# Attention and two feed-forward layers on one core: the order of an attention round written anew on every engine queue

## The chip, the cores and the metric

One core of a Trainium2 chip runs the whole program in one launch. The metric is the device time of a run in microseconds (us); lower is better. The kernel before takes 1006.01 us, the median of three runs.

## What is computed

Causal attention with a decay over 4 batches of 8 heads, 576 positions, 64 values a head, then two feed-forward layers over the 2304 tokens. All in float32, so most products are made of three (high times high, high times low, low times high).

```python
scores = (1 / 8) * q @ k.T                      # per head, 576 x 576
cum = cumsum(log(clip(f, 1e-4, 1)))
scores = where(causal, -1e9, scores + cum[:, None] - cum[None, :])
attn = exp(scores - max) ; attn = attn / (sum(attn) + 1e-9)
x = attn @ v                                    # as (2304, 512)
h = x @ w_in ; x = (h * cos(h)) @ w_out         # layer one, 512 -> 2048 -> 512
y = (silu(x @ w_gate) * (x @ w_val)) @ w_out2   # layer two, 512 -> 1536 -> 512
```

## The kernel before, in words

The program has three stages on one set of engines: attention, layer one, layer two. The change touches attention and the seam to layer one.

Attention works on 16 pairs of heads (index i), both heads of a pair side by side in the partitions (e = 0, 1). The 576 positions are cut into five tiles of queries t: 128 each, 64 in the last. Each pair passes through small steps, which the text names as the program's table does:

- `q0` to `q3` (emit_q, L117 and L114, POOL): split q and k of the pair into a rounded high part and the rest, into the tile xq. `qb` (emit_b) lays a block diagonal bd for tile 4 and a selector that adds the decay.
- `S4, S1, S2, S0, S3` (emit_s, L412 to L421, PE): score products of a tile into the PSUM tiles sA (S4, later S0 and S2 together) and sB (S1, later S3). The last product of each adds the decay: its weights are the selector, its moving side the cumulated logarithms cs.
- `M` (emit_m, L436, DVE): masks the scores, takes them out of PSUM into P (tile 4: Q), and gives the row maximum. M40 is that of tile 4. `E` (emit_e, L444, ACT): exponential with the row's sum.
- `T0` to `T3` (emit_t, L481, PE): transposes of the probabilities into a PSUM tile t; there are two such tiles. `C` (emit_c, L502 on ACT, L500 on DVE): copies out of it to pt. Which copies are DVE's is the table CPD.
- `ra, rb, rt, rc, rd, re, rf` (emit_recip): the reciprocal of the sums, transposed, to DRAM (r_d) and read back over all partitions (rs).
- `V0, V1` (emit_pv, L535, PE): probabilities times values, one half of the columns each, into the two halves of one t tile. `N0, N1` (emit_n, L544, DVE): times the reciprocals. `xo`: the result to DRAM.
- `wd, w1` to `w7` (w_load, w_step): prepare one weight tile of layer one in each round, beside attention. w1 is an absolute value on ACT (L167), w2 a clamp (L169), w3 two shifts (L171), w4 and w5 put the bits together (L173, L175), w6 rounds on POOL (L117) and w7 takes the rest on POOL (L114).

What sets the order is one string, SCH: a list such as `M40@1`, which means that in round n the step M40 of pair n - 1 stands here. The loop at the end of attention runs through the list once a round (21 rounds), and `in_order` fixes that every engine keeps the order in which its instructions were recorded. So each engine has a fixed queue, and a step that waits holds all that stands behind it on its engine. FIRST and AHEAD give the first pairs another order. A t tile becomes free when its readers are done; a wait for it is a wait for the whole tile.

Layer one (in1, out1) begins behind attention: for each of 16 blocks j of the hidden size a product h (L252, 12 matmuls), a cosine over ACT and DVE, and two steps later the product with w_out (L694). Its first block of tokens is loaded and split (xh, xl) on POOL in the last rounds: XL, XP and XN say when and how many splits at a time.

Of the kernel before, what the change touches and what calls it, by code (L numbers as in the profile page):

```python
# [9 lines left out]
F32 = mybir.dt.float32  # L10
F32R = mybir.dt.float32r
# [15 lines left out]
CH = 384  # L27
# [69 lines left out]
def body(ctx: ExitStack, tc: tile.TileContext, qk, v, f, w_in, w_out, w_gate, w_val, w_out2, mask_c, ident_c, sel_c, out):  # L97
# [56 lines left out]
    def w_step(n, k):  # L154

        raw, ta = wcur[n][:2]
        w32 = raw.bitcast(I32).rearrange("p (c two) -> p c two", two=2)
        lo, hi = w32[:, :, 0], w32[:, :, 1]  # L160
        if k == 1:
            sp = stages[0] if n < SA else stages[1]
            while n >= SB and held[0] > TAB2 - 2:
                small.pop(0)[1]()
            ta = wcur[n][1] = sp.tile([128, 512], I32, tag="ta", name="ta", bufs=TAB if n < SA else TAB2)
            hi32 = raw.bitcast(F32).rearrange("p (c two) -> p c two", two=2)[:, :, 1]
            ACT.activation(out=ta.bitcast(F32), in_=hi32, func=AF.Abs)  # L167
        elif k == 2:
            DVE.tensor_scalar(out=ta.bitcast(F32), in0=ta.bitcast(F32), scalar1=HI_MIN, scalar2=HI_MAX, op0=ALU.max, op1=ALU.min)  # L169
        elif k == 3:  # L170
            DVE.tensor_scalar(out=ta, in0=ta, scalar1=5, scalar2=2, op0=ALU.logical_shift_left, op1=ALU.logical_shift_right)  # L171
        elif k == 4:
# [215 lines left out]
    def s_place(i, t):  # L388
        if i < 2 and t in (1, 4):
# [8 lines left out]
    def emit_s(i, t):  # L398
        s = sels[i % 3]
        if i > 1 or i == 1 and t in (1, 4):  # L400
# [5 lines left out]
        if t < 4:  # L406
# [11 lines left out]
        for m, (x, y) in enumerate([*((x, y) for _, y, x in p), (s[:, 64:192], None)]):  # L418
            for g in range(2):
# [30 lines left out]
    def emit_recip(i, k):  # L450
# [42 lines left out]
    def emit_c(i, g, e):  # L493
# [10 lines left out]
        n = 4 - g  # L504
        if g < 2:
# [3 lines left out]
        for e in range(2):  # L509
            if g == 2:  # L510
                copy(o[:, e, PJ[g]:PJ[g] + 128 * n].rearrange("p (n h x) -> p n h x", n=n, h=2),
                     ps[:, :, 64 * n * e:64 * n * e + 64 * n].rearrange("p h (n x) -> p n h x", n=n))
        if g == 3:
# [44 lines left out]


    def op(o, i):  # L560

        if not 0 <= i < NPAIR:
            return
        if i in FIRST and o[0] in "SME":
            now = [int(t[0]) for t in FIRST[i].split()]
            slot = [4, 1, 2, 0, 3]
            k = slot.index(int(o[1]))
            if o[0] == "S":
                o = f"S{now[k]}"
            else:  # L570
                flat = {x: [f"{t}{e}" for t in x for e in range(2 if t != 4 else 1)] for x in (tuple(now), tuple(slot))}
                o = o[0] + flat[tuple(now)][flat[tuple(slot)].index(o[1:])]
        if (o, i) in BEHIND:
# [58 lines left out]

    sch = [t.split("@") for t in SCH.split()]
# [481 lines left out]
```

## Time and profile before

| | |
|---|---|
| three runs | 1004.76, 1006.01, 1006.56 us |
| the profiled execution | 1007.36 us |
| its span, first to last instruction | 1005.6 us |
| busy: PE, DVE, ACT, POOL | 96%, 74%, 51%, 46% of the span |
| mean granted clock of TensorE | 0.983 of 2.4 GHz |
| attention | about the first 205 us |

The shares are means over three stages. From 211 us on PE runs without a gap; the idle time of PE lies in attention, so that stage is to be read by itself, by rounds.

### The profile page before, as it was taken

Reading aid. Unit: us, or ns where it says so; the run is one execution under the profiler, and the core shown is the slowest. Engines: PE = TensorE matmul, PEld = TensorE weight load, DVE = VectorE, ACT = ScalarE, POOL = GpSimd, SP = SyncE. Lnnn points to the kernel's source line nnn. Section 1 sums busy time; section 2 is a strip of 40 time slices with the busy share of each in tenths; the row PEclk is TensorE's granted clock in tenths of the full one; section 3 lists DMA queues with packets and bytes.
Section 4 is the critical chain, followed back from the end, with each engine's and each line's share of the span. In section 5 each row is a group of like instructions: output and inputs, shape, how many; then the busy total and the mean of one; then the engine's idle time right before and its main releaser. Section 6 shows DMA issues by size and latency. Waiting matters only on the chain.

```text
span 1005.6 us, 18021 instructions
## 1 busy us (share of the span) xinstructions
PE 960.7 (96%) x6522; PEld 903.7 (90%) x6522; DVE 744.8 (74%) x1311; ACT 507.9 (51%) x1122; POOL 466.8 (46%) x493
## 2 busy tenths in 40 slices
PE   8777878899999999999999999999999999999998
PEld 5666666599999999999999999999999999988888
DVE  6678777679788876979886653768576676898884
ACT  6767677645554555655655542324232331455552
POOL 7566665344225667769788002545553554200000
PEclk9989899899999999999999999999999999999999
DMA  4545443543345875967966776132961318954531
GB/s 160 178 161 196 158 171 128 174 156 129 105 147 189 251 219 179 302 211 239 290 226 219 252 251 223 55 118 78 350 219 56 118 48 312 363 188 138 157 105 43
DMA packets 108985, 182.61 MB, mean 182 GB/s; under 512 B 8912, under 2 KB 72800, under 8 KB 108896
## 3 DMA queue, kind: packets, MB, share of 16 engines
q1 hardware_dynamic: 108896, 181.46, 54.6%
q8 instruction: 51, 0.84, 0.3%
q14 instruction: 38, 0.31, 0.1%
HBM read 118.43 MB, written 62.99 MB: 180 GB/s over the span
## 4 chain that ended last, share of the span: by engine, by line
PE 79%; DVE 9%; DMA 4%; POOL 3%; issue 3%; ACT 2%; SPq 0%; DVEq 0%; POOLq 0%; ACTq 0%
PE h L252 15%; PE t L694 14%; PE b L885 11%; PE c L885 7%; PE a L885 7%; PE t L535 5%; PE b L974 5%; PE a L974 3%; DVE P L436 3%; PE sA L421 2%; PE c L974 1%; PE d L974 1%; PE sA L412 1%; DMA xl<-x 1%; PE t L481 1%
## 5 line engine op out<-in xcount | busy, mean ns | idle before, releaser
L252 PE MATMUL h<-xh,w 128*128 128x384 f32 x768 | 149.9, 335 | 1.5 <-POOL xh L117 1.5
L694 PE MATMUL t<-gh,w 128*128 128x384 f32 x704 | 137.1, 335 | 1.2 <-DVE part L704 0.9
L252 PEld LDWEIGHTS h<-xh,w 128*128 128x128 f32 x768 | 134.7, 188 | 2.3 <-POOL xh L117 1.9
L694 PEld LDWEIGHTS t<-gh,w 128*128 128x128 f32 x704 | 122.9, 188 | 2.8 <-DVE part L704 1.9
L885 PE MATMUL b<-c,wu 128*128 128x384 f32 x648 | 121.1, 334 | 0.0
L670 ACT ACTIVATE n<-h 128x384 int32<-128x384 f32 x96 | 47.2, 491 | 139.1 <-PE h L252 132.2
L885 PEld LDWEIGHTS b<-c,wu 128*128 128x128 f32 x648 | 113.1, 188 | 0.0
L672 DVE SCALAR_TENSOR_TENSOR r<-h,n 128x384 f32<-128x384 f32 x96 | 53.2, 554 | 74.0 <-ACT n L670 73.9
L848 POOL TENSOR_TENSOR s<-u,s 128x384 f32<-128x384 f32 x33 | 37.8, 1146 | 123.6 <-ACT s L847 117.1
L535 PE MATMUL t<-pt,vt 128*64 128x320 f32 (+4 forms) x448 | 61.6, 423 | 33.4 <-DVE xp L544 27.4
L535 PEld LDWEIGHTS t<-pt,vt 128*64 128x64 f32 x448 | 35.0, 157 | 59.4 <-DVE xp L544 31.3
L252 PE MATMUL h<-xl,w 128*128 128x384 f32 x384 | 82.0, 334 | 0.0
L885 PE MATMUL c<-c,wu 128*128 128x384 f32 x432 | 80.7, 334 | 0.0
L885 PE MATMUL a<-c,wu 128*128 128x384 f32 x432 | 80.7, 334 | 0.0
L885 PEld LDWEIGHTS c<-c,wu 128*128 128x128 f32 x432 | 75.4, 188 | 0.0
L885 PEld LDWEIGHTS a<-c,wu 128*128 128x128 f32 x432 | 75.4, 188 | 0.0
L694 PE MATMUL t<-gl,w 128*128 128x384 f32 x352 | 75.2, 334 | 0.0
L114 POOL TENSOR_TENSOR w<-ta,w 128x512 fp32r<-128x512 f32 x32 | 44.9, 1403 | 57.6 <-ACT w L189 29.4
L502 ACT COPY pt<-t 128x256 f32<-128x256 f32 (+2 forms) x109 | 42.4, 449 | 56.3 <-PE t L481 55.5
L444 ACT ACTIVATE P<-P,mx 128x384 f32<-128x384 f32 (+3 forms) x128 | 70.1, 549 | 0.2 <-DVE mx L436 0.2
L252 PEld LDWEIGHTS h<-xl,w 128*128 128x128 f32 x384 | 67.9, 188 | 0.0
L173 DVE SCALAR_TENSOR_TENSOR ta<-wraw,ta 128x512 int32<-128x512 int32 x68 | 66.0, 970 | 0.5
(160 smaller groups left out, 2113.4 us busy)
## 6 DMA issues: line engine op xcount, KB each, us to landing
wu<-wu SPq DMA_DIRECT2D x63, 512.0 KB, 5.0
wraw<-in_w_out_dram SPq DMA_DIRECT2D x28, 512.0 KB, 3.6
wu<-hi SPq DMA_DIRECT2D x54, 256.0 KB, 4.2
gd<-g SPq DMA_DIRECT2D x72, 192.0 KB, 2.4
gt<-gd SPq DMA_DIRECT2D x36, 384.0 KB, 5.7
raw<-in_qk_dram SPq DMA_DIRECT2D x16, 576.0 KB
wu<-sums SPq DMA_DIRECT2D x36, 256.0 KB, 3.3
xb<-x SPq DMA_DIRECT2D x24, 384.0 KB, 7.7
```

Source lines behind the costliest of these rows:

```text
L114: eng.tensor_tensor(out=o, in0=a, in1=b.bitcast(F32), op=ALU.subtract)
L173: DVE.scalar_tensor_tensor(out=ta, in0=lo, scalar=29, in1=ta, op0=ALU.logical_shift_right, op1=ALU.bitwise_or)
L252: PE.matmul(ps, lhsT=w[:, a, 128 * kk:128 * kk + 128], rhs=b[:, kk], start=(n == 0), stop=(n == 3 * KD - 1))
L444: ACT.activation(out=o, in_=o, func=AF.Exp, scale=-1.0, bias=mxt[p % 8][:, t:t + 1], accum_out=smt[p // 2 % 3][:, c:c + 1])
L502: ACT.copy(out=o, in_=x)
L535: PE.matmul(ps[64 * e:64 * e + 64, o:min(w, o + KW[j])], lhsT=vt_t[i][:, j, e], rhs=PT[i][:, e, c:c + w - o], start=(j == 0), stop=(j == b ...
L670: ACT.activation(out=n, in_=h, func=AF.Copy, scale=INV2PI, bias=0.25)
L672: DVE.scalar_tensor_tensor(out=r, in0=h, scalar=INV2PI, in1=n, op0=ALU.mult, op1=ALU.subtract)
L694: PE.matmul(acc[m][:, :CH], lhsT=wo[:, q, 128 * m:128 * m + 128], rhs=x, start=(j == a and n == 0), stop=False)
L848: e.tensor_tensor(out=s, in0=C[:, 0], in1=s, op=ALU.mult)
L885: PE.matmul(d, lhsT=wu[q, i][1][:, mem, x, 128 * kt:128 * kt + 128], rhs=r, start=bool(s and n == 0), stop=(n == 5), skip_group_check=True)
L974: PE.matmul(ot[:, :w], lhsT=cmb[i][:, x, q], rhs=m[:, 256 * y:256 * y + w], start=(i in (1, 5) and n == 0), stop=(n == len(ops) - 1), skip ...
```

## The change

Five things are changed together. (1) SCH is written anew: the same steps in another order, with other offsets (V and C30 one round earlier against the rest, N behind both halves of V, 20 rounds in place of 21); FIRST and AHEAD follow. (2) The clamp w2 goes from DVE to POOL for the weights prepared within attention. (3) Copy C21 goes from ACT to DVE (CPD). (4) The decay's selectors are no longer laid out per pair as 64x128 columns: one small tile holds a column per pair and head, and the products read it with step 0. Only tile 4 gets a laid out selector (sf, one POOL instruction). (5) The products h of layer one for j = 0 and j = 1 are issued ahead of T1 and V0 of the last pair, in PSUM that the scores have left; the splits of the first tokens start earlier for it.

```diff
-CPD = ("10", "11")
-SCH = "ld@-1 rd@3 xo@5 M30@2 M31@2 T0@3 q0@0 C00@3 C01@3 V0@4 w2@4 w3@4 q1@0 ...
+CPD = ("10", "11", "21")
+XH = {("T1", NPAIR - 1): 0, ("V0", NPAIR - 1): 1}
+SCH = "M21@2 w4@4 M31@2 q2@0 w5@4 N0@4 E30@2 ld@-1 N1@4 S4@1 T1@3 E00@2 re@3 rf@3 ...
...
-XL = 13
-XP = 14
-XN = 2
+XL = 10
+XP = 11
+XN = 1
...
         elif k == 2:
-            DVE.tensor_scalar(out=ta.bitcast(F32), in0=ta.bitcast(F32), scalar1=HI_MIN, ...
+            (POOL if n < SA else DVE).tensor_scalar(out=ta.bitcast(F32), in0=ta.bitcast(F32), scalar1=HI_MIN, ...
...
-    sels = [ap1.tile([128, 256], F32R, name=f"sel{k}") for k in range(3)]
+    sel = ap1.tile([128, NPAIR, 2], F32R, name="sel")
+    sel4s = [ap1.tile([128, 128], F32R, name=f"sf{k}") for k in range(2)]
...
-            pool_round(s[b, 128 * e:128 * e + 128], selr[b, i:i + 1].to_broadcast([64, 128]))
+        if i == 0:
+            for e in range(2):
+                b = slice(64 * e, 64 * e + 64)
+                pool_round(sel[b, :, e], selr[b, :NPAIR])
+        pool_round(sel4s[i % 2].rearrange("p (e x) -> p e x", e=2), sel[:, i, :, None].bitcast(F32).to_broadcast([128, 2, 64]))
...
-                PE.matmul(o[:, e], lhsT=s[b, 128 * e:128 * e + 128], rhs=cs[b, :ext], start=False, stop=True)
+                PE.matmul(o[:, e], lhsT=sel[b, i, e:e + 1].to_broadcast([64, 128]), rhs=cs[b, :ext], start=False, stop=True)
...
+    def ahead(j):
+        if "h" not in pools:
+            pctx.close()
+            pools["h"] = hctx.enter_context(tc.tile_pool(name="ps_h", bufs=4, space=PSUM))
+        h = hs[0, j] = pools["h"].tile([128, 512], F32, tag="h", name="h")[:, :CH]
+        mm_in(h, wt["i", j], xs[0])
...
     for n in range(NPAIR + moff):
         for o, off in sch:
+            if (o, n - int(off)) in XH:
+                ahead(XH[o, n - int(off)])
             op(o, n - int(off))
```

What stands where in a steady round, on three engines. First PE, at the values (V, the rows with pt and vt) of one pair, with the engines on whose semaphore a row waits. Before:

```order
L535 MATMUL t<-pt,vt 64x256 [waits DMAHW6_49,PE_49,Activation_49]
L535 MATMUL t<-pt,vt 64x256
L535 MATMUL t<-pt,vt 64x128 x2
L535 MATMUL t<-pt,vt 64x320 [waits DVE_49]
L535 MATMUL t<-pt,vt 64x320 x5
L535 MATMUL t<-pt,vt 64x192 x2
L535 MATMUL t<-pt,vt 64x64 x2
L421 MATMUL sA<-xq,bd_119 128x288 [waits Pool_49]
```

Now:

```order
L533 MATMUL t<-pt,vt 64x256 [waits DMAHW2_49,DVE_49,Activation_49]
L533 MATMUL t<-pt,vt 64x256
L533 MATMUL t<-pt,vt 64x128 x2
L533 MATMUL t<-pt,vt 64x320 x6
L533 MATMUL t<-pt,vt 64x192 x2
L533 MATMUL t<-pt,vt 64x64 x2
L423 MATMUL sA<-xq,bd_118 128x288 [waits DVE_49,Pool_49]
```

The second half (64x320 and on) waited for DVE and now waits for nothing; the wait for DVE stands at the first half and at S4 (the row with bd) behind it.

Second DVE, at the same place of the round (xp is N, ta the weight, the rows with mask are M, Q is M40). Before:

```order
L436 ISA P_110,mx_172<-sB,mask 128x512
L436 ISA mx_172 128x1
L169 TENSOR_SCALAR ta<-ta 128x512
L171 TENSOR_SCALAR ta<-ta 128x512
L544 TENSOR_TENSOR xp<-t,rs 128x256
L173 SCALAR_TENSOR_TENSOR ta<-wraw,ta 128x512
L544 TENSOR_TENSOR xp<-t,rs 128x320
L175 SCALAR_TENSOR_TENSOR ta<-wraw,ta 128x512
L436 ISA Q_116,mx_173<-sA,mask_99 128x576
```

Now:

```order
L438 ISA P_110,mx_170<-sA,mask 128x384
L438 ISA mx_170 128x1
L174 SCALAR_TENSOR_TENSOR ta<-wraw,ta 128x512
L438 ISA P_110,mx_170<-sB,mask 128x512
L438 ISA mx_170 128x1
L176 SCALAR_TENSOR_TENSOR ta<-wraw,ta 128x512
L542 TENSOR_TENSOR xp<-t,rs 128x256
L542 TENSOR_TENSOR xp<-t,rs 128x320
L438 ISA Q_116,mx_171<-sA,mask_99 128x576
```

The clamp is gone from DVE, w3 stands earlier in the round (behind the two M of tile 1), w4 and w5 stand ahead of N0, and N0 and N1 follow each other directly.

Third POOL, one round (rc is ra, ta the clamp, xq the splits of q and k, sel and sf the selectors). Before:

```order
L454 TENSOR_SCALAR rc_179<-sm_176 128x9
L117 TENSOR_SCALAR w_1969<-ta 128x512
L117 TENSOR_SCALAR sel_120<-selr 64x128 x2
L117 TENSOR_SCALAR bd_118<-xq 64x2x64 x2
L114 TENSOR_TENSOR w_1969<-ta,w_1969 128x512
L114 TENSOR_TENSOR xq<-raw,xq 128x576
L117 TENSOR_SCALAR xq<-raw 128x576
```

Now:

```order
L456 TENSOR_SCALAR rc_177<-sm_174 128x9
L170 TENSOR_SCALAR ta<-ta 128x512
L115 TENSOR_TENSOR xq<-raw,xq 128x576 x2
L118 TENSOR_SCALAR sf_121<-sel 128x128
L118 TENSOR_SCALAR bd_118<-xq 64x2x64 x2
L115 TENSOR_TENSOR w_872<-ta,w_872 128x512
L118 TENSOR_SCALAR xq<-raw 128x576 x2
L118 TENSOR_SCALAR w_1047<-ta 128x512
```

The clamp stands between ra and the two long splits; the selector is one instruction in place of two; the round of w (w6) stands at the end, ahead of the next ra.

## Rows read from the trace of the kernel before

**Rows 1.** The page, part 1: busy us, share of the span, instructions.

```profile
PE 960.7 (96%) x6522; PEld 903.7 (90%) x6522; DVE 744.8 (74%) x1311; ACT 507.9 (51%) x1122; POOL 466.8 (46%) x493
```

**Rows 2.** Busy time by stretch: length, five engines, PEclk, DMA share, GB/s.

```profile
42.70:163.15 120.45, 96.15 (x1201) 76.06 (x1201) 92.08 (x271) 84.86 (x273) 76.26 (x110) 0.93 0.49 166
114.96:127.83 12.87, 10.36 (x121) 8.12 (x121) 9.32 (x28) 8.58 (x29) 7.70 (x12) 0.87 0.46 160
127.83:138.99 11.16, 8.84 (x120) 7.21 (x120) 9.07 (x28) 8.36 (x28) 7.56 (x11) 1.00 0.56 192
...
178.45:211.28 32.83, 27.37 (x290) 20.33 (x291) 20.19 (x49) 16.99 (x48) 14.57 (x17) 0.90 0.46 153
```

**Rows 3.** Waits, 42.70 to 163.15 us: total, times, longest us.

```profile
POOL w L117 <- DVE ta L175: 23.7, 10, 3.4
PE t L535 <- DVE xp L544: 23.5, 11, 2.6
DVE xp L544 <- PE t L535: 23.3, 10, 3.3
```

**Rows 4.** Timeline of PE: start, us, instruction, count, idle before and releaser.

```profile
114.96 3.33 PE L535 MATMUL t<-pt,vt 128*64 128x320 f32 x20 [2.40 <-DVE xp L544]
...
127.83 2.28 PE L535 MATMUL t<-pt,vt 128*64 128x320 f32 x20 [2.50 <-DVE xp L544]
...
135.85 0.87 PE L535 MATMUL t<-pt,vt 128*64 128x256 f32 x8
```

**Rows 5.** Groups of DVE by shape, 42.70 to 163.15: busy us, mean ns, idle.

```profile
L171 DVE TENSOR_SCALAR ta<-ta 128x512 int32<-128x512 int32 x10 | 12.2, 1216 | 0.3
L500 DVE COPY pt<-t 128x384 f32<-128x384 f32 x20 | 10.1, 546 | 0.0
L173 DVE SCALAR_TENSOR_TENSOR ta<-wraw,ta 128x512 int32<-128x512 int32 x11 | 8.3, 751 | 0.0
L169 DVE TENSOR_SCALAR ta<-ta 128x512 f32<-128x512 f32 x10 | 7.9, 791 | 0.0
...
L175 DVE SCALAR_TENSOR_TENSOR ta<-wraw,ta 128x512 int32<-128x512 int32 x10 | 6.8, 682 | 0.0
```

**Rows 6.** Timelines of DVE (two rows) and POOL (the last), two rounds.

```profile
137.10 1.51 DVE L171 TENSOR_SCALAR ta<-ta 128x512 int32<-128x512 int32 x1
...
174.06 0.43 DVE L171 TENSOR_SCALAR ta<-ta 128x512 int32<-128x512 int32 x1
...
136.77 1.55 POOL L114 TENSOR_TENSOR xq<-raw,xq 128x576 fp32r<-128x576 f32 x1
```

**Rows 7.** Groups of POOL by shape, 40 to 180 us.

```profile
L117 POOL TENSOR_SCALAR w<-ta 128x512 fp32r<-128x512 f32 x12 | 7.5, 622 | 27.5 <-DVE ta L175 27.5
...
L117 POOL TENSOR_SCALAR sel<-selr 64x128 fp32r<-64x128 f32 x22 | 6.5, 295 | 0.7
```

**Rows 8.** Groups of weight loads by shape, 42.70 to 163.15 us.

```profile
L415 PEld LDWEIGHTS sA<-cs,sel 64*128 64x128 f32 x40 | 3.9, 186 | 0.0
```

**Rows 9.** Timeline of DVE where the first pair's values are done.

```profile
29.60 0.42 DVE L544 TENSOR_TENSOR xp<-t,rs 128x256 f32<-128x256 f32 x1 [1.76 <-DMA rs<-r_d]
33.88 0.49 DVE L544 TENSOR_TENSOR xp<-t,rs 128x320 f32<-128x320 f32 x1 [3.85 <-PE t L535]
35.28 0.76 DVE L436 CUSTOM_DVE_ANT_0 Q<-sA,mask 128x576 f32<-128x576 f32 x1 [0.92 <-PE sA L421]
```

**Rows 10.** The seam: timelines of DVE and PE, then POOL's splits (groups, 0 to 260).

```profile
178.45 0.76 DVE L436 CUSTOM_DVE_ANT_0 Q<-sA,mask 128x576 f32<-128x576 f32 x1 [0.17 <-PE sA L421]
...
205.45 1.14 PE L252 MATMUL h<-xh,w 128*128 128x384 f32 x5
...
211.28 1.61 PE L694 MATMUL t<-gh,w 128*128 128x384 f32 x8
...
L114 POOL TENSOR_TENSOR xl<-xl,xh 128x384 fp32r<-128x384 f32 x8 | 8.9, 1107 | 0.7
...
L117 POOL TENSOR_SCALAR xh<-xl 128x384 fp32r<-128x384 f32 x8 | 5.8, 721 | 11.5 <-DMA xl<-x 11.5
```

More of the change, by code (lines that the diff above doesn't have):

```diff
@@ L43 @@
 WHE = 1
-CPD = ("10", "11")
-FIRST = {0: "2 0 3 1 4", 1: "2 0 3 4 1"}
-SCH = "ld@-1 rd@3 xo@5 M30@2 M31@2 T0@3 q0@0 C00@3 C01@3 V0@4 w2@4 w3@4 q1@0 E20@2 E21@2 N0@4 E00@2 E01@2 w4@4 V1@4 E30@2 N1@4 E31@2 w1@3 w5@4 q2@0 S4@1 re@3 rf@3 ra@2 S1@1 M40@1 T3@3 M10@1 C30@3 M11@1 T1@3 rb@2 S2@1 C10@3 E40@1 C11@3 w6@4 S0@1 wd@2 lv@3 T2@3 rt@2 M20@1 C20@3 S3@1 rc@2 E10@1 M21@1 qb@0 E11@1 M00@1 w7@4 M01@1 q3@0 xk@3"
+CPD = ("10", "11", "21")
+FIRST = {0: "20314", 1: "32041"}
+XH = {("T1", NPAIR - 1): 0, ("V0", NPAIR - 1): 1}
+SCH = "M21@2 w4@4 M31@2 q2@0 w5@4 N0@4 E30@2 ld@-1 N1@4 S4@1 T1@3 E00@2 re@3 rf@3 q0@0 S1@1 xo@4 wd@2 E01@2 E10@2 M40@1 w6@4 T3@3 E21@2 E31@2 C10@3 S2@1 C11@3 w1@3 ra@2 S0@1 w2@3 q3@0 rb@2 M10@1 M11@1 T2@3 rt@2 C30@3 w3@3 q1@0 qb@0 C21@3 E40@1 T0@2 S3@1 rc@2 C20@3 rd@2 M20@1 M01@1 M00@1 C01@2 M30@1 V0@3 E11@1 V1@3 E20@1 w7@4 lv@2 C00@2 xk@3"
 JS = 9
@@ L168, in w_step @@
         elif k == 2:
-            DVE.tensor_scalar(out=ta.bitcast(F32), in0=ta.bitcast(F32), scalar1=HI_MIN, scalar2=HI_MAX, op0=ALU.max, op1=ALU.min)
+            (POOL if n < SA else DVE).tensor_scalar(out=ta.bitcast(F32), in0=ta.bitcast(F32), scalar1=HI_MIN, scalar2=HI_MAX, op0=ALU.max, op1=ALU.min)
         elif k == 3:
@@ L320, in body @@
     POOL.memset(mask4[:, 0:512], 0.0)
-    for b in (*sels, bd0, *bd):
+    for b in (bd0, sel, *bd):
         POOL.memset(b.bitcast(F32), 0.0)
@@ L363, in emit_q @@
     def emit_q(i, k):
-        if k == 0:
+        if i not in xq:
             xq[i] = aps.tile([128, 2, 2, S], F32R, tag="xq", name="xq", bufs=2)
@@ L388, in s_place @@
     def s_place(i, t):
-        if i < 2 and t in (1, 4):
+        if i == 0 and t in (1, 4) or i == 1 and t == 4:
             if (i, t) not in early:
@@ L414, in emit_s @@
                 b = slice(64 * e, 64 * e + 64)
-                PE.matmul(o[:, e], lhsT=s[b, 128 * e:128 * e + 128], rhs=cs[b, :ext], start=False, stop=True)
+                PE.matmul(o[:, e], lhsT=sel[b, i, e:e + 1].to_broadcast([64, 128]), rhs=cs[b, :ext], start=False, stop=True)
             return
         o = s_place(i, 4)
-        for m, (x, y) in enumerate([*((x, y) for _, y, x in p), (s[:, 64:192], None)]):
+        for m, (x, y) in enumerate([*((x, y) for _, y, x in p), (sel4s[i % 2], None)]):
             for g in range(2):
@@ L457, in emit_recip @@
         elif k == "t":
-            rps[i] = (tps[i - 1, 2][:9, :, 256:320] if i else t_tile()[:9, :, :64])
+            rps[i] = tps[i - 1, 2][:9, :, 256:320] if i else tps[0, 1][:9, :, 384:448]
             for h in range(2):
@@ L504, in emit_c @@
         n = 4 - g
-        if g < 2:
+        if g < 3:
             copy(o[:, e, PJ[g]:PJ[g] + 128 * n].rearrange("p (n h x) -> p n h x", n=n, h=2),
@@ L508, in emit_c @@
             return
[L509 to L512, printed above, removed]
         if g == 3:
@@ L557, in load_chunk, with flat @@
             xs[c] = load_x(xpools[c % 2], x1v, c % 2 * HT + c // 2 * CH, CH, GX and c == 1, later)
+    sch = [t.split("@") for t in SCH.split()]
+    SLOTS = {k: [t for _, _, t in sorted((int(f), n, t) for n, (t, f) in enumerate(sch) if t[0] == k)] for k in "SME"}
+    def flat(k, ts):
+        return [t + e for t in ts for e in ([""] if k == "S" else "0" if t == "4" else "01")]
     def op(o, i):
@@ L564, in op @@
         if i in FIRST and o[0] in "SME":
[L565 to L572, printed above, removed]
+            o = o[0] + flat(o[0], FIRST[i])[SLOTS[o[0]].index(o)]
         if (o, i) in BEHIND:
@@ L577, in op @@
         act(o, i)
-    AHEAD = {("M10", 1): (("ra", 0), ("rb", 0)), ("S4", 2): (("rt", 0), ("rc", 0), ("rd", 0)), ("T2", 0): (("re", 0), ("rf", 0))}
+    AHEAD = {("M10", 1): (("ra", 0), ("rb", 0)), ("C10", 0): (("rt", 0), ("rc", 0), ("rd", 0)), ("T0", 1): (("re", 0), ("rf", 0))}
     BEHIND = {a for b in AHEAD.values() for a in b}
@@ L631, in in_order @@
             last_[ins.engine] = ins
-    sch = [t.split("@") for t in SCH.split()]
+    def ahead(j):
[4 more added lines that the diff above has]
+        mm_in(h, wt["i", j], xs[0])
+    pools, hs = {}, {}
     moff = max(int(o) for _, o in sch)
@@ L651, in body @@
     stages[1] = rctx.enter_context(tc.tile_pool(name="stage2", bufs=RWB2, side=SIDE_R))
-    ps_h = hctx.enter_context(tc.tile_pool(name="ps_h", bufs=4, space=PSUM))
     G = {}
@@ L662, in in1 @@
         if k == 0:
-            h = ps_h.tile([128, 512], F32, tag="h", name="h")[:, :CH]
-            mm_in(h, wt["i", j], xs[c])
+            h = hs.pop((c, j), None)
+            if h is None:
+                h = pools["h"].tile([128, 512], F32, tag="h", name="h")[:, :CH]
+                mm_in(h, wt["i", j], xs[c])
             n = mp2.tile([128, CH], I32, tag="n", name="n")
```

5 lines of the change are left out of this document (removed).

## The prediction

> **What bounds the kernel now.** I read the page first: PE is busy for 96% of the span [rows 1]. That is a mean over three stages, so I cut attention into its rounds, from one start of V1 to the next. Ten rounds take 120.45 us, 12.05 each, and in them PE is busy for 9.6, DVE 9.2, ACT 8.5 and POOL 7.6 us a round [rows 2]. No engine is full; something goes round in a circle. The waits name it: PE's V1 waits for DVE's N0, 23.5 us in all, and DVE's N1 waits for V1, 23.3 us [rows 3], some 2.35 us a round each. The place in the queues explains it. V1 writes the second half of the tile that N0 reads, and was recorded behind N0; N0 stands behind all M of the round and the weight steps w2 and w3. So PE stands still until DVE has drained its list, then DVE stands still while PE does V1, S4 and so on. The round is the sum of both.
>
> The rounds come in two lengths, 11.16 and 12.9 us [rows 2]. In the long one V1 took 3.33 us in place of 2.28 [rows 4], and the granted clock of the round was 0.87, that is, part of it ran at 1.2 GHz in place of 2.4. Both had PE idle for about 2.4 us right before. A second thing lies in the weight steps: L171 took 0.43 us in one round and 1.51 in another, where POOL was inside a 1.55 us split that began 0.33 us earlier [rows 6]. It ended when that split had ended. DVE's instructions that only touch SBUF (L169, L171, L173, L175) and POOL's exclude each other. In the mean L171 costs 1.22 us and L169 0.79 [rows 5].
>
> **The change, part by part.**
>
> *The order of V and N.* In the new queue V1 stands directly behind V0 and waits for nothing, as the order shows. PE's own work is then one stretch: 8.84 us in a round at the full clock [rows 2]. The 2.35 us of waiting on each side go. What is late next? I add up each engine. PE: 8.84. ACT: 8.49, less one copy of about 0.38, 8.1. DVE: 9.21, less L169 (0.79), plus the copy C21. That copy has no row on DVE; between 0.27 (half of one of 128x384, 0.546 [rows 5]) and 0.55 I take 0.38, in proportion with a fixed part. That makes 8.8, of which 0.8 is L171 waiting for POOL (1.22 less 0.43).
>
> *The clamp on POOL, the selectors.* A POOL instruction of the same size and kind takes 0.622 us; two selector instructions of 0.295 go and one comes, which I take as the same 0.3 (128 partitions in place of 64, as many columns) [rows 7]. POOL: 7.63 + 0.62 - 0.29 = 7.96 us.
>
> *What DVE and POOL share.* Since their SBUF instructions exclude each other, they add: 7.96 of POOL, 0.43 of w3, 0.75 of w4 and 0.68 of w5 [rows 5, 6], 9.8 us. In the kernel before POOL stood idle for 2.4 us a round until w5 came [rows 3], and w5 ran in that gap for nothing; in the new round the gap is nearly gone. POOL's 7.96 holds some 0.3 of such waiting itself, so the floor lies between 9.5 and 9.8. It is the highest of all the sums, above PE's 8.84. A little waiting of POOL stays, as ra needs the last exponential and the clamp needs w1 of the same round. I take 9.9 us a round, with 9.4 and 10.9 as its ends. The Trainium skill has the rule (SBUF — State Buffer, section SBUF: two separate sides): the port pair of DVE and GpSimd is an exclusive lock, held for the whole instruction, and the other "fully blocks". By that rule, which the rows on L171 agree with, moving the clamp to POOL is no relief of the shared part; without it the sum would be PE's 8.84, the first rival below.
>
> *The rounds.* M40 of pair 3 starts at 35.28 us [rows 9] and M40 of pair 15 at 178.45 [rows 10]: twelve rounds of 11.93. Twelve of 9.9 save 24.4 us. Two of them also carry a split of the first tokens while q and k are still split, 0.72 + 1.11 us of POOL [rows 10]; I charge 1.0 in all, between 0 and 3.7. Net 23.4.
>
> *The first rounds.* M40 of pair 3 stood behind N1, which waited 3.85 us for V1, and V1 for N0, which waited for the reciprocals from DRAM until 29.60; then S4 came, 0.92 [rows 9]. Now V1 and S4 do not wait for N0. If the reciprocals land as before, N0 and N1 are done at about 30.4 and M40 follows. The order of ACT and POOL puts the row of reciprocals about 1 us later, so I take 31.4, between 30.4 and 35.28: 3.9 us saved.
>
> *The seam.* From M40 of pair 15 to the first product with w_out 32.83 us pass, with PE busy for 27.37 at a mean clock of 0.90 [rows 2, 10]. At 0.90 a fifth of the time ran at half the rate, so the work is 27.37 - 3.3 = 24.1 us at the full clock. Before, 33 matmuls of h stood behind the last values, 5.83 us [rows 10]; the order now has 31 of 36 ahead of V0 or inside the earlier waits of PE, and five behind V1. Two waits stay: the last exponentials before T0 and V of pair 14, and the copies C10 and C11 of pair 15, which on DVE stand behind the first step of layer one. I take 27.5, between 24.1 and 32.83: 5.3 us saved.
>
> *Selectors with step 0.* The loads are as many as before, eight a round for four tiles, at 186 ns, in the shadow of PE's products [rows 8]. No row has a load with step 0. The bounds are 0 and 8 x 0.19 = 1.5 us a round (each twice as long, nothing hidden); a gain is excluded, since nothing waits for them now. I take 0, as weight loads are busy for only 76 of 120 us [rows 2].
>
> *After the seam* nothing is changed; PE has no gap there and sets the pace.
>
> The sum: 23.4 + 3.9 + 5.3 = 32.6 us off the profiled execution, 1007.36, gives 974.8. That execution is 1.35 us above the median of the runs, 1006.01; from the median it is **973.4 us**.
>
> **The rivals.**
>
> *A. The lock does not bind.* w3, w4 and w5 fall into moments in which POOL waits for ACT or DVE, as L175 does now (0.68 in the mean, hardly a wait [rows 5]). Then PE sets the round with 8.84, say 8.9: twelve rounds save 12.0 more, 961.4. For it: POOL still has three places where it waits. Against it: only 1 to 2 us of a round would be left to POOL, and w3 meets the two long splits. 13%.
>
> *B. The lock and the queues bite harder.* w3 on DVE needs the clamp on POOL of the same round, and behind w3 stand C21, which V0 awaits, and five M. If w3 and w4 each wait for a whole split of 1.4 to 1.5 us, or the clock falls in part of the rounds as now, a round takes about 11.2: 989.0. For it: L171 waits for POOL in most rounds already (mean 1.22 against 0.43). 16%.
>
> *C. The rounds do not shorten.* Another circle of waits, say through POOL and ACT (last exponential, clamp, w3, M20, its exponential), takes the place of the one removed. Its steps add up to about 7 us, too little for 11.93, so it needs DMA or a tile that I overlooked. Only the ends gain, 996.8; and if they fail too, no change. 4%, of which half within the bound.
>
> *D. Slower.* PE becomes the bound at the low clock. V1 takes 3.33 to 4 us when it falls, 1.5 to 1.75 times [rows 4]. A round wholly at 1.2 GHz would take some 8.84 x 1.75 = 15.5. The ends save 8.2 net of the splits, so the kernel is slower by over 2 us only if rounds take 12.8 or more, that is, if 60% of PE's work runs at the low level. A case of 13 gives about 1011. For it: the clock was below full for part of half of the rounds. Against it: the slow V1 came behind 2.4 us without work [rows 4], and the new round leaves gaps of 1 us or less. 5%.
>
> **How the numbers follow.** The forecast holds 62%: 973.4, and with its round between 9.4 and 10.9 it runs from 967 to 985. The range takes in A at one end and B with a margin at the other, 961 to 992, and leaves out C, D and what lies beyond. About 0.2%, 2 us, is what a measurement can tell, since the three runs lie 1.8 us apart. Faster: forecast, A, B and half of C, 93%. Within the bound: 2%. Slower: D, 5%.
>
> **What would show it.** In the new profile: V1 of a steady round directly behind V0, with no idle time of PE by DVE's N; a round of 9.4 to 10.4 us between two V1; L172 (w3) still near 1.2 us and POOL busy for over 80% of a round; the granted clock at 1.00 in most rounds; M40 of pair 3 near 31 us; the first product with w_out near 179 us (31.4 + 12 x 9.9 + 1.0 + 27.5 = 178.7), against 211.28. Wrong would be: PE idle for over 1.5 us ahead of V0 or S4, waiting for DVE (B); DVE without a wait and PE with none either (A); V1 at 3 us or more round after round (D).

## The result, and the profile after

The changed kernel takes 995.61 us (median of four runs, 992.61 to 996.58), against 1006.01: a ratio of 0.989, 95% interval 0.987 to 0.992. That is faster by 1.1%, a third of what was forecast (973.4), and outside the range of 961 to 992. The profiled execution, the fastest of the four, took 992.61 us with a span of 990.5; its sum is made against the 1007.36 and 1005.6 of before.

Five points cut the span: M40 of pair 3 [rows 9], M40 of pair 15 [rows 10], the first product with w_out [rows 10] and the third, then the end.

| stretch, us | before | forecast | after |
|---|---|---|---|
| start to M40 of pair 3 | 35.28 | 31.4 | 31.51 |
| to M40 of pair 15, 12 rounds | 143.17 | 119.8 | 127.96 |
| to the first product with w_out | 32.83 | 27.5 | 31.57 |
| to the third (before: 219.67) | 8.39 | 8.39 | 14.81 |
| to the end of the span | 785.9 | 785.9 | 784.7 |

The first rounds came as forecast. The rounds fell short by 8.2 us, the seam by 4.1, and then 6.4 were lost where nothing was expected at all. The border between rounds and seam moves from one execution to the next, though. Here V0 and V1 of pair 12, just ahead of M40 of pair 15, took 4.61 us in place of 2.92, at a granted clock of 0.84 in that round. In e10, below, the same kernel once more, they took 2.92, while M40 of pair 3 came 1.2 us later; there the rounds take 125.16 us and the seam 34.26. The sum is the same, 159.5 and 159.4. So the rounds were 5.4 to 8.2 us longer than forecast and the seam 4.1 to 6.8. The rows for the table: timelines of DVE and PE of the changed kernel, answering to [rows 9, 10].

```profile
31.51 0.76 DVE L438 CUSTOM_DVE_ANT_0 Q<-sA,mask 128x576 f32<-128x576 f32 x1 [0.42 <-PE sA L423]
...
145.97 0.74 DVE L438 CUSTOM_DVE_ANT_0 Q<-sA,mask 128x576 f32<-128x576 f32 x1
159.47 0.76 DVE L438 CUSTOM_DVE_ANT_0 Q<-sA,mask 128x576 f32<-128x576 f32 x1 [0.43 <-PE sA L423]
...
153.56 4.61 PE L533 MATMUL t<-pt,vt 128*64 128x256 f32 x28 [2.45 <-ACT pt L504]
...
191.04 1.55 PE L699 MATMUL t<-gh,w 128*128 128x384 f32 x8
...
198.84 2.93 PE L699 MATMUL t<-gh,w 128*128 128x384 f32 x8 [3.47 <-ACT gh L683]
...
205.85 1.55 PE L699 MATMUL t<-gh,w 128*128 128x384 f32 x8
```

Now a steady round. The windows from V0 to V0, the columns those of [rows 2]:

```profile
99.81:110.26 10.45, 8.64 (x120) 6.97 (x121) 9.33 (x28) 8.07 (x27) 9.95 (x12) 1.00 0.61 197
110.26:120.72 10.46, 8.64 (x120) 6.95 (x120) 9.33 (x28) 8.08 (x27) 9.95 (x12) 1.00 0.60 196
```

A round takes 10.46 us. In these two the clock is at 1.00, V0 and V1 run back to back in 2.92 us, and no wait between V and N is left. But POOL is busy for 9.95 where 7.96 was reckoned. Its groups (60 to 150 us) show the place, against [rows 7]:

```profile
L170 POOL TENSOR_SCALAR ta<-ta 128x512 f32<-128x512 f32 x9 | 17.3, 1926 | 1.5 <-ACT ta L168 1.4
...
L118 POOL TENSOR_SCALAR w<-ta 128x512 fp32r<-128x512 f32 x9 | 5.6, 617 | 0.0
```

The clamp (L170) takes 1.93 us. The multiply-and-add of the same shape, from whose row it was priced, still takes 0.62. What this holds up, in the waits from 42.7 to 150 us, answering to [rows 3]:

```profile
ACT row L465 <- DVE pt L502: 22.1, 10, 2.4
...
PE t L533 <- ACT pt L504: 16.4, 9, 1.8
DVE ta L172 <- POOL ta L170: 10.2, 9, 1.1
POOL ta L170 <- ACT ta L168: 1.9, 10, 0.3
```

Read from the bottom it is one chain. POOL waits for w1 on ACT and clamps. DVE waits 1.1 us for the clamp before w3 (L172). Behind w3 stands C21 (L502); the row of reciprocals (L465) and C20 (L504) read the same tile of PSUM, and by its waits ACT takes them up only when C21 is done. V0 (L533) waits for C20, and PE stands still for 1.8 us a round. The timeline of one such round, POOL, DVE, ACT and PE:

```profile
116.20 1.93 POOL L170 TENSOR_SCALAR ta<-ta 128x512 f32<-128x512 f32 x1 [0.18 <-ACT ta L168]
118.09 2.96 POOL L115 TENSOR_TENSOR xq<-raw,xq 128x576 fp32r<-128x576 f32 x2
...
118.16 1.63 DVE L172 TENSOR_SCALAR ta<-ta 128x512 int32<-128x512 int32 x1 [1.13 <-POOL ta L170]
119.71 0.41 DVE L502 COPY pt<-t 128x256 f32<-128x256 f32 x1
...
120.15 0.25 ACT L465 COPY row<-t 9x128 f32<-9x128 f32 x1 [2.38 <-DVE pt L502]
120.31 0.83 ACT L504 COPY pt<-t 128x256 f32<-128x256 f32 x2
...
120.72 0.65 PE L533 MATMUL t<-pt,vt 128*64 128x256 f32 x4 [1.82 <-ACT pt L504]
```

The lock of [rows 6] is here as well: POOL's xq split began 0.07 us before w3, and w3 took 1.63 us in place of 0.43.

### The profile page after: what moved, and what is told of

It is laid out like the page before. It is cut to its first block, busy times and chain, and to the rows that moved or that the text cites. A ratio compares the mean times of both kernels' runs of the same rounds, so it can differ in the third digit from the quotient of the medians.

```text
span 990.5 us, 18044 instructions
## 1 busy us (share of the span) xinstructions
PE 949.6 (96%) x6522; PEld 897.8 (91%) x6522; DVE 747.9 (76%) x1312; ACT 502.2 (51%) x1106; POOL 496.8 (50%) x492
## 4 chain that ended last, share of the span: by engine, by line
PE 72%; DVE 3%; issue 2%; POOL 2%; DMA 1%; ACT 0%; SPq 0%; DVEq 0%; POOLq 0%; ACTq 0%
PE h L253 17%; PE t L699 16%; PE b L890 11%; PE c L890 8%; PE a L890 8%; PE b L979 5%; PE a L979 3%; PE c L979 1%; PE d L979 1%; PE t L702 1%; DVE c L115 1%; DMA xl<-x 1%; POOL sums L115 1%; DVE gs L764 0%; DVE ta L174 0%
## 5 line engine op out<-in xcount | busy, mean ns | idle before, releaser
L115 POOL TENSOR_TENSOR w<-ta,w 128x512 fp32r<-128x512 f32 x32 | 48.8, 1524 | 62.4 <-DVE ta L172 31.3
L533 PEld LDWEIGHTS t<-pt,vt 128*64 128x64 f32 x448 | 32.0, 147 | 46.8 <-ACT pt L504 28.6
L533 PE MATMUL t<-pt,vt 128*64 128x320 f32 (+4 forms) x448 | 51.7, 386 | 22.7 <-ACT pt L504 22.6
L446 ACT ACTIVATE P<-P,mx 128x256 f32<-128x256 f32 (+3 forms) x128 | 70.2, 550 | 0.2 <-DVE mx L438 0.2
L172 DVE TENSOR_SCALAR ta<-ta 128x512 int32<-128x512 int32 x68 | 56.3, 828 | 14.3 <-POOL ta L170 13.8
L679 ACT ACTIVATE r<-r,hpi 128x384 f32<-128x384 f32 x96 | 59.5, 619 | 10.6 <-DVE r L677 10.5
```

Of the source, the lines that this page charges most:

```text
L115: eng.tensor_tensor(out=o, in0=a, in1=b.bitcast(F32), op=ALU.subtract)
L446: ACT.activation(out=o, in_=o, func=AF.Exp, scale=-1.0, bias=mxt[p % 8][:, t:t + 1], accum_out=smt[p // 2 % 3][:, c:c + 1])
L533: PE.matmul(ps[64 * e:64 * e + 64, o:min(w, o + KW[j])], lhsT=vt_t[i][:, j, e], rhs=PT[i][:, e, c:c + w - o], start=(j == 0), stop=(j == b ...
L679: ACT.activation(out=r, in_=r, func=AF.Sin, bias=hpi, scale=float(2 * np.pi))
```

## Experiments

All runs e1 to e12 (there is no e3) were timed against the kernel before on the same chip; e13 has one execution. "Round" is the mean from V0 to V0 over six to eight rounds of the profiled execution. The diffs are given in short form.

| run | time, us | ratio to before, 95% | round, us |
|---|---|---|---|
| the change | 995.61 | 0.989 (0.987 to 0.992) | 10.46 |
| e10, the change again | 995.80 | 0.990 (0.988 to 0.992) | 10.46 |
| e1, clamp on DVE | 985.96 | 0.981 (0.978 to 0.984) | 9.88 |
| e2, multiply and add for the clamp | 977.59 | 0.973 (0.969 to 0.977) | 9.16 |
| e4, gate two steps later | 988.70 | 0.984 (0.980 to 0.987) | 10.46 |
| e5, w3 in the next round | 985.89 | 0.981 (0.978 to 0.984) | 10.18 |
| e6, no products ahead | 989.06 | 0.984 (0.982 to 0.986) | 10.46 |
| e7, before with the clamp on POOL | 1041.64 | 1.038 (1.035 to 1.040) | 14.18 |
| e8, w6 on ACT | 1000.35 | 0.995 (0.994 to 0.997) | 10.96 |
| e9, w3, w6 and gate together | 974.32 | 0.971 (0.968 to 0.973) | 9.75 |
| e11, e9 without products ahead | 979.02 | 0.973 (0.970 to 0.975) | 9.76 |
| e12, e9 with half the clamps on DVE | 969.32 | 0.963 (0.961 to 0.966) | 9.04 |
| e13, max without min (one execution) | 995.37 | none | 10.46 |

### The price of the clamp (e2, e13, e1, e7)

**e2.** The same order with a cheap instruction in the clamp's place.

```diff
-POOL.tensor_scalar(ta, ta, HI_MIN, HI_MAX, op0=max, op1=min)
+POOL.tensor_scalar(ta, ta, 1.0, 0.0, op0=mult, op1=add)
```

> Leaves the clamp of the first 15 weight blocks out: POOL multiplies by one and adds zero in its place, same tile, same shape, same order, same waits. Price theory (the forecast had everything right but the clamp's 0.62 us on POOL): the instruction takes 0.62 instead of 1.93, w3 starts about 1.1 earlier, the round falls from 10.45 to 9.3 to 9.6, the time by 12 x 0.85 to 12 x 1.15 = 10 to 14, to 979 to 983. Rival (the two-port lock between w3 and the xq splits and C21 behind it bind by themselves): the lock simply catches w3 at another xq split, round 10.1 or more, time 988 to 992.

The round fell by 1.30 us, the instruction by 1.31: one for one, and a little further than the price theory's 9.3 to 9.6. So the price alone kept the rounds from the forecast. Group of POOL (60 to 150 us) and window (42.70 to 142 us) of e2:

```profile
L170 POOL TENSOR_SCALAR ta<-ta 128x512 f32<-128x512 f32 x9 | 5.6, 619 | 1.5 <-ACT ta L168 1.3
...
42.70:142.00 99.30, 92.32 (x1262) 73.61 (x1262) 97.95 (x291) 86.45 (x279) 94.79 (x119) 1.00 0.65 218
```

DVE is busy for 97.95 of 99.30 us: with the cheap clamp DVE becomes the bound, its waiting for the lock included.

**e13.** Is it the two operations, or the form?

```diff
-op0=max, op1=min, scalar2=HI_MAX
+op0=max, op1=add, scalar2=0.0
```

> Changed kernel with the upper bound of the clamp of the first 15 blocks left out: POOL does max and then adds zero, same tile and form. If each of max and min has a price of its own over that of multiply and add (1.93 against 0.62 for two), the instruction takes about 1.27 and the round falls by about 0.65; if the operation max alone puts the whole instruction at the slow rate, it takes 1.9 and nothing changes.

```profile
L170 POOL TENSOR_SCALAR ta<-ta 128x512 f32<-128x512 f32 x9 | 17.4, 1931 | 1.4 <-ACT ta L168 1.3
```

1.93 us again: one max is enough to put the whole instruction at the slow rate. Min alone was not tried.

**e1.** Only the clamp's engine is undone.

```diff
-(POOL if n < SA else DVE).tensor_scalar(...max, min)
+DVE.tensor_scalar(...max, min)
```

> Changed kernel with step 2 of the first 15 weight blocks (the clamp) back on DVE, at the same place of the order. Full-POOL theory (in the changed kernel's rounds POOL is busy 9.95 of 10.45 us and the clamp is 1.93 of it, so POOL itself, and through it w3, C21 and the row copy, sets the round): POOL falls to about 8.0 and stops binding; on DVE the clamp costs 0.5 to 0.8 (0.79 mean before), w3 starts at about 117.8 where it started at 118.16, so the round falls by about 0.4 to near 10.05 and the time by 12 x 0.4 = 5 to about 988. Rival (the port lock binds, whichever engine has the clamp): DVE's work of 9.33 grows by 0.8 to 10.1 and a second two-port step waits for an xq split, round 10.4 to 10.9, time 993 to 998.

The round fell by 0.58 to 9.88, and the time to a ratio below the change's interval. So that part of the change is a loss by itself: the new order without it is the better kernel. Of the rival something holds too: DVE is now busy without a break (windows of e1, 80.00 of 80.00 us). On DVE the clamp met POOL's splits and took 1.52 us here (0.44 in e12), and w3 behind it then 0.88. Groups of DVE in e1, 60 to 150 us:

```profile
L170 DVE TENSOR_SCALAR ta<-ta 128x512 f32<-128x512 f32 x9 | 13.7, 1517 | 0.0
...
L172 DVE TENSOR_SCALAR ta<-ta 128x512 int32<-128x512 int32 x9 | 7.9, 875 | 0.0
...
68.00:148.00 80.00, 71.58 (x964) 56.82 (x964) 80.00 (x230) 65.33 (x211) 65.07 (x85) 1.00 0.63 208
```

**e7.** The kernel before with this one part, the edit of e1 the other way round.

> The kernel before with the clamp alone on POOL, nothing else changed. Price-and-queue theory (1.93 us on POOL instead of 0.79 on DVE, w3 right behind it on DVE, and N0, for which V1 waits, behind w3 and w4): N0 comes 1.1 to 1.6 later, the round grows from 11.93 to 13.0 to 13.5, the time by 14 to 21 to 1018 to 1027. Rival (a place where POOL has 4.4 us of a round to spare takes the clamp for nothing, and DVE gains 0.8): round 11.4 to 11.9, time 999 to 1005.

The sign was as price-and-queue theory had it, the size twice as large: rounds of 14.18 in place of 11.93. POOL had over 4 us of a round to spare there and it did not help. Waits of e7, the whole span:

```profile
PE t L535 <- DVE xp L544: 42.2, 15, 3.9
...
DVE ta L171 <- POOL ta L169: 24.0, 13, 5.9
```

w3 waits for the clamp, N0 stands behind w3, V1 behind N0. PE's wait for N0 was 27.4 us over the whole span before, so it grew by 1.0 us a round, near the 1.1 to 1.6 charged. Part of the rest I had not charged: V1, which comes after that wait, took 3.1 to 4.3 us in nearly every round, at a granted clock of 0.76 to 0.88, where before it was 3.33 and 2.28 in turn [rows 4]. That is 0.8 us more a round in the mean (3.7 against 2.9).

### What holds the round (e5, e8, e9, e12)

POOL is full in a round (9.95 of 10.46) and there is also a chain through the clamp. Which of them binds?

**e5.** w3 leaves the chain; POOL keeps all its work.

```diff
-SCH = "M21@2 w4@4 ... C30@3 w3@3 q1@0 qb@0 C21@3 ...
+SCH = "M21@2 w3@4 w4@4 ... C30@3 q1@0 qb@0 C21@3 ...
```

> Changed kernel with only w3 moved: from ahead of C21 to the start of the next round, ahead of w4, so that nothing in DVE's queue waits for the clamp of the same round; the clamp stays on POOL. Full-POOL theory: V0 no longer waits behind w3, but POOL still has 9.95 to 10.2 us of work a round, so the round falls only to 10.1 to 10.3 and the time by 2 to 4, to 988 to 991. Rival (the place of w3, that is the chain clamp, w3, C21, row copy, C20, V0, costs the 1.8 us that V0 waits): round 9.2 to 9.7, time 977 to 983.

The round is the full-POOL theory's, 10.18. PE no longer waits for ACT but for bd, which POOL writes (waits, 42.7 to 150 us):

```profile
PE sA L423 <- POOL bd L118: 12.7, 10, 1.4
```

The time fell to 985.89, between the ranges of the two theories, and further than these rounds explain (12 x 0.28 = 3.4 us). The rest lies in three rounds in which POOL has less to do: from V0 of pair 1 to that of pair 3 two rounds of 8.66 and 9.27 us (10.44 and 10.45 in the change), and from pair 13 to pair 14 one of 7.35 (10.26 in the change). POOL is busy for 6.12, 8.86 and 5.76 us in them. Timeline of PE in e5:

```profile
39.27 2.92 PE L533 MATMUL t<-pt,vt 128*64 128x256 f32 x28
...
47.93 2.93 PE L533 MATMUL t<-pt,vt 128*64 128x256 f32 x28
...
160.88 2.92 PE L533 MATMUL t<-pt,vt 128*64 128x256 f32 x28
...
168.23 4.61 PE L533 MATMUL t<-pt,vt 128*64 128x256 f32 x28
```

**e8.** Now 0.62 us are taken from POOL, the chain is left.

```diff
-if WHE and n < SA: pool_round(w, ta)
+if WHE and n < 0: pool_round(w, ta)
```

So ACT.copy does it.

> Changed kernel with step 6 of the weights (the copy w from ta, 0.617 us on POOL) on ACT; the clamp stays on POOL at 1.93. Full-POOL theory: any 0.62 taken from POOL shortens the round as much as 0.62 off the clamp would, ACT (8.1 of 10.45 busy) has the room: round 9.8 to 9.9, time 7 to 8 shorter than the changed kernel's. Rival (only the chain through the clamp, w3 and C21 counts, and step 6 is not in it): round 10.3 to 10.45, time within 2.

Both were wrong: slower than the change, 10.96 a round. Timelines of ACT and POOL in e8:

```profile
107.35 0.60 ACT L190 CAST w<-ta 128x512 fp32r<-128x512 f32 x1
...
109.18 0.64 ACT L168 ACTIVATE ta<-wraw 128x512 f32<-128x512 f32 x1
...
109.35 0.25 POOL L456 TENSOR_SCALAR rc<-sm 128x9 f32<-128x9 f32 x1 [1.03 <-ACT P L446]
109.90 1.93 POOL L170 TENSOR_SCALAR ta<-ta 128x512 f32<-128x512 f32 x1 [0.30 <-ACT ta L168]
```

The copy on ACT stands ahead of two exponentials and of w1. They come 0.5 us later, POOL waits 1.03 + 0.30 us for them, and the round is 0.5 longer. So the full-POOL theory falls for the change as it is. What binds is a loop over three engines: row, C20, the exponentials and w1 on ACT, the clamp on POOL, w3 and C21 on DVE, then the row of the next round. From the clamp to the row it takes 3.95 us (116.20 to 120.15), and from the row to the next clamp ACT needs the other 6.5. ACT has no gap on that way: in ten rounds it waits for C21 (22.1 us) and once for PE (1.6). So the 0.6 us that e8 put there came out as 0.5 a round. POOL's load lies only 0.28 us below (e5), so it looked like the bound.

PE is not in that loop. In one round of the change V0 and V1 took 4.61 us, at a granted clock of 0.84, and the next V0 came after 10.45 us like the others, without its wait:

```profile
47.53 4.61 PE L533 MATMUL t<-pt,vt 128*64 128x256 f32 x28 [1.80 <-ACT pt L504]
```

**e9.** If so, both have to be moved: w3 off the loop first, then w6 off POOL, and to a place on ACT behind the last wide exponential. The gate's edit (e4 below) is in it.

```diff
-SCH = "M21@2 w4@4 M31@2 ... w6@4 ... E31@2 C10@3 ... w3@3 ...
+SCH = "M21@2 w3@4 w4@4 M31@2 ... E31@2 w6@4 C10@3 ...
```

> Changed kernel with three edits together: w3 at the start of the next round, step 6 of the weights on ACT (behind the round's last exponentials of the 512-wide tile), and the second chunk's load two steps later. If POOL's work sets the round, the effects add: round 10.18 - 0.62 = 9.56, so 12 x 0.62 = 7.4 less than with w3 moved alone, and 5.8 less for the gate: 972 to 977. If they overlap (DVE's 8.8 to 9.4 us with the locks, or ACT's new place, becomes the bound): round 9.9 or more, 977 to 981.

974.32, within the first case; the round is 9.75, 0.2 above the sum. It beats the change, and e5 as well.

**e12.** The clamp of every second block of e9 on DVE (`n % 2`).

> The combined kernel with the clamp of every second block back on DVE. Its rounds of 9.76 are held by POOL (PE waits for bd, 14.9 us in 12 times; POOL busy 76.7 of 80 us). Load theory: POOL falls by 0.97 a round on the mean, DVE (73.6 of 80 us) grows by 0.4 to 0.8, the mean round comes to 9.4 to 9.6, the time 2 to 4 less than the combined kernel's. Rival (the clamp on DVE meets the two-port lock, 1.5 us as in the kernel with all clamps on DVE, and DVE becomes the bound of those rounds): 0 to 3 longer.

969.32, the best kernel of the study, more than expected: rounds alternate between 8.6 and 9.5. On DVE the clamp took 0.44 (x5, 60 to 150 us): it fell between POOL's splits. In the window from 42.70 to 142 us PE, DVE, ACT and POOL are each busy for 93 to 96%:

```profile
42.70:142.00 99.30, 93.34 (x1292) 75.21 (x1287) 94.78 (x299) 95.35 (x298) 92.82 (x104) 1.00 0.67 223
```

### The seam (e4, e6, e10, e11)

PE's idle 3.47 us before the second product with w_out (first fence above) have their cause on DVE. Timeline of DVE, then the queue of SP, of the changed kernel:

```profile
197.66 0.14 DVE L144 CAST xl<-gs 1x1 fp32r<-1x1 f32 x1 [6.66 <-issue]
197.73 0.54 DVE L681 TENSOR_TENSOR h<-h,r 128x384 f32<-128x384 f32 x1
...
187.71 0.33 SPq L152 DMA_DIRECT2D wraw<-in_w_in_dram  x1
...
189.03 0.43 SPq L152 DMA_DIRECT2D wraw<-in_w_out_dram  x1
191.03 0.33 SPq L547 DMA_DIRECT2D x<-xp  x1
```

L144 is the gate that load_chunk(1) puts on DVE. It writes into memory that attention has left. I take it that it waits for the last store of x, which was issued at 191.03 behind four weight loads of 512 KB: the profile names no releaser here (issue), but in e6 below it names that store for the same instruction. For 6.66 us DVE did nothing, with the second h x r (L681) behind the gate. PE ran out of work, and went on at the 1.2 GHz level (granted clock 0.50 from 198.84 to 201.77: 2.93 us for eight matmuls that take 1.55).

**e4.** The gate, its load and the four splits come two steps of the layer later (j == 4, XS = 5).

```diff
-... or c == 0 and j == 2 and 1 not in loaded:
+... or c == 0 and j == 4 and 1 not in loaded:
```

> Changed kernel with the load of the second chunk (and the gate ahead of it on DVE) two steps of layer one later, and its four splits from step 5 on. Gate theory (the gate stood 6.66 us at the head of DVE for the last x store and held the second h x r, so PE idled 3.47 us and then ran about 3 us longer at the 1.2 GHz level): the store has landed when the gate comes, both vanish, time 985 to 988. Rival 1 (the wait only passes to the next instruction that needs the freed memory): 991 to 993. Rival 2 (the lower clock there has another cause, only the idle 3.47 goes): 989.

The third product with w_out came at 199.81 in place of 205.85, 6.0 us earlier; idle time and low clock both went. The second one in e4:

```profile
195.65 1.55 PE L699 MATMUL t<-gh,w 128*128 128x384 f32 x8
```

The time, 988.70, lies just above the gate theory's range and next to rival 2's 989; the trace is what rules rival 2 out, as the eight matmuls take 1.55 us again. The span fell by 4.4 only. What comes behind the third product took 786.3 us against 784.7 in the change, but 788.6 in e10, the change again, so that no loss can be read from it.

**e6.** No products ahead, the gate left as it is.

```diff
-XH = {("T1", NPAIR - 1): 0, ("V0", NPAIR - 1): 1}
+XH = {}
```

> Changed kernel without the two products of layer one ahead of the last values; the third pool of PSUM is opened after the last round instead. Given-back theory (the 2 x 2.2 us that the two products gain are taken back by the gate's 3.47 us idle and the 3 us at the 1.2 GHz level behind it): without them the first out product comes about 4.4 later, but the store of the last pair has then nearly landed when the gate is reached, PE idles there less than 1 us, and the time is within 2 us of the changed kernel's. Rival (the products are a true gain and the gate's stall has nothing to do with them): the stall stays at 3 to 4 us and the time is 4 to 5 longer than the changed kernel's.

Better than the theory: not the same but faster than the change, which e10, the change on another chip, confirms.

> The changed kernel itself once more, beside the others on one chip: both theories expect its ratio of 0.987 to 0.992 to the kernel before again, 991 to 996 us. If the kernel without the two products ahead is truly faster than it, as given-back theory has it (and by more: those products cost net), this run lies 4 to 6 us above that kernel's 0.984; if the two were the same and the chips differed, it comes out at 0.984 too.

So this part of the change, too, is a loss as it stands. Windows from V0 of pair 14 to the first product with w_out, of the change and of e6:

```profile
174.35:191.04 16.69, 15.46 (x126) 11.99 (x127) 8.08 (x16) 6.82 (x14) 6.55 (x6) 0.90 0.28 98
```

```profile
176.52:192.75 16.23, 15.06 (x126) 12.06 (x127) 8.39 (x16) 7.04 (x15) 6.52 (x6) 0.92 0.46 154
```

PE is idle for 1.2 us in either: where the products stand, there was nothing to fill. PE's idle time of the seam lies ahead of it. From M40 of pair 15 to V0 of pair 14 PE is idle for 4.6 us in the change and 4.8 in e6:

```profile
159.47:174.35 14.88, 10.31 (x164) 8.10 (x164) 12.09 (x33) 9.63 (x32) 9.96 (x11) 0.88 0.48 154
```

```profile
161.41:176.52 15.11, 10.31 (x164) 8.10 (x165) 12.31 (x33) 9.80 (x33) 10.10 (x12) 0.86 0.48 152
```

The products only put V of pair 15 off (from 183.55 to 187.21), and with it the last store, which then meets the gate. In e6 the gate waits 3.02 us for that store, and PE never stands still for it (8.32 us from the first product with w_out to the third, without a gap):

```profile
195.50 0.14 DVE L144 CAST xl<-gs 1x1 fp32r<-1x1 f32 x1 [3.02 <-DMA x<-xp]
```

**e11.** With the gate out of the way, are they worth something?

> The combined kernel (w3 in the next round, step 6 on ACT, second chunk's load two steps later) without the two products of layer one ahead of the last values. Nothing-to-fill theory (in the last rounds PE had little idle time for the products to fill, they only delay the last values: from V0(14) to the first out product 16.69 us with them and 16.23 without, with no gate between): within 1.5 us of the combined kernel, either way. Rival (they are worth the 4 to 5 us of the forecast once the gate no longer takes them back): 3 to 5 us longer than the combined kernel.

0.973 against 0.971 for e9, on two chips: 2 us in their favour, with intervals that overlap and don't rule out the rival's 3. The traces say less: from V0 of pair 14 to the third product with w_out e9 takes 25.28 us and e11 25.81. So the products are worth 0.5 us there; the rival's 3 to 5 are not in that stretch. Timelines of PE, e9 and then e11:

```profile
165.64 4.73 PE L533 MATMUL t<-pt,vt 128*64 128x256 f32 x28
...
190.92 1.55 PE L699 MATMUL t<-gh,w 128*128 128x384 f32 x8
```

```profile
165.47 4.66 PE L533 MATMUL t<-pt,vt 128*64 128x256 f32 x28
...
191.28 1.55 PE L702 MATMUL t<-gh,w 128*128 128x384 f32 x8
```

## Why the prediction was wrong, point by point

**What held.** The circle of V1 and N0 was the bound before, and the new queue undid it: in ten rounds one wait of 1.0 us between them is left. The clock stayed up in most rounds (1.00; 0.84 in the rounds behind V0 of pairs 2 and 12). M40 of pair 3 was forecast at 31.4 and came at 31.51; in e10, where V0 and V1 of pair 0 took 3.87 us (granted clock of that round 0.90), it came at 32.72. The loads with step 0 still take 186 ns (L417, x36), and nothing waits for them. POOL busy for over 80%: it was 95%.

**The step that failed first** is "A POOL instruction of the same size and kind takes 0.622 us". Size and place were right, the kind was not: the row was a multiply and add, the clamp is max and min, and takes 1.93. With the instruction at the price I gave (e2), the kernel takes 0.973 of before: 978.9 against the forecast of 973.4, well inside the range. That it comes so near is luck in part: the twelve rounds of e2 took 110.9 us (M40 at 30.42 and 141.28), 8.9 less than the forecast's 119.8, and made up for the seam and what follows it, 9.3 more than forecast. No row of the kernel before had max or min on POOL, so this term needed bounds (the same operation on DVE, 0.79, the same form on POOL, 0.62, and an upper one); it was given a single value.

**The mechanism** of the longer round was written down as rival B: "w3 on DVE needs the clamp on POOL of the same round, and behind w3 stand C21, which V0 awaits". It was priced by two waits for the lock and given 16%. The runs show the same path from the clamp to V0 with another cause: the clamp's own time (e2), carried round a loop that closes over ACT (e8), not over PE. The sign that the text named for B, PE idle over 1.5 us ahead of V0, is there (1.82), though it waits for ACT, behind DVE.

**The floor of the lock**, "9.8 us", fell too, in the other direction. With the cheap clamp a round is 9.16 us, below the 9.5 that was its lower end: the durations hold more waiting than the 0.3 I took off, which stands in no row. In e2 POOL is busy for 8.73 us a round, and w3, w4 and w5 take 1.53, 0.68 and 1.11, together 12.1 in a round of 9.16. If the two exclude each other, what each waits for the other is counted on both sides, and such busy times can't be added up to a floor. How much of each is waiting no run shows. As for the rule of the Trainium skill (SBUF — State Buffer, SBUF: two separate sides) that the lock is held for the whole instruction, the rows agree in kind: beside a split w3 took 1.63 us, and the clamp on DVE 1.52, where alone they took 0.43 and 0.44.

**The rounds with the first tokens' splits** were charged 1.0 us. The last one took 13.50 us, 3.0 above a steady one, in the profiled execution. Of these 1.7 are V0 and V1 at the low clock: in e10 it took 11.94, 1.5 above. The round from V0 of pair 11 to that of pair 12, 11.91 us, shows where that goes: POOL is busy for 11.42 of it.

**The seam**, "5.3 us saved", was 1.3, and in e10 it was 1.4 longer than before. The working put 31 matmuls "ahead of V0 or inside the earlier waits of PE". The waits are still there, 5.5 us of idle time of PE in the seam before, 5.8 in the change and 6.0 in e6, but the matmuls could not go into them. Most of the waits come ahead of V0 of pair 14 (3.9, 4.6 and 4.8 us), and the products stand behind it, where PE was idle for 1.6 us before and is for 1.2 now, with them or without.

**"After the seam nothing is changed"** was the costliest sentence after the first: 6.4 us. The diff is empty there, but the gate waits for the last store. Before, 33 matmuls of h stood behind the last values and covered it; with two of three blocks issued ahead that cover was gone (e4, e6). A second thing was lost with the new order: before, the last store was issued ahead of the four weight loads (the second of the two below, at 206.1), and the gate at 211.70 did not wait. In the change and in e6 the store stands behind them. Queue of SP and gate, before:

```profile
199.30 7.10 SPq L549 DMA_DIRECT2D x<-xp  x2
208.77 0.33 SPq L151 DMA_DIRECT2D wraw<-in_w_in_dram  x1
...
211.70 0.13 DVE L143 CAST xl<-gs 1x1 fp32r<-1x1 f32 x1
```

No run moves the store ahead of the loads, so how the loss is shared between the two is open.

**Not tried by themselves** were C21 on DVE and the selectors. C21 lies in the loop, behind w3.

## What to carry to other kernels

Price a moved instruction by a row with the same operation on the same engine; shape and form are not enough, and where no such row exists the term is a range. Before moving a step to the engine with the most idle time, follow who waits for it in the same round: an engine that is idle for a quarter or a third of the time can still lie in the loop that sets the round (ACT in e8, POOL in e7). Work that is issued ahead into idle time has to be priced against the idle time that comes behind its place in the queue, and whatever it used to cover further on has to be looked up.

## What the runs showed of the hardware

Not expected: TENSOR_SCALAR on POOL, 128x512 in float32, takes 1.93 us with max and min, 1.93 with max and add, and 0.62 with multiply and add. On DVE max and min took 0.40 to 0.44 where nothing was in the way (198.66 in the change, e12). An instruction that waited for a store of 288 KB, issued behind four loads of 512 KB, was released 6.6 us after the store's issue (188.92 to 195.50 in e6, where the profile names the store; 191.03 to 197.66 in the change).
